# A fused adaLN block on one core: other DMA order, halos off GpSimd, wider value products, and DMA transposes instead of TensorE transposes

## The chip, the core and the metric

The kernel runs on one core of a Trainium2 chip. The core has TensorE (PE), whose results go to PSUM; VectorE (DVE) and ScalarE (ACT), which read PSUM and SBUF; GpSimd (POOL); and SyncE (SP), which here issues nearly all DMAs. Each engine works through its own list of instructions in order, and waits on semaphores for the others. A DMA is issued by an engine's queue and carried out by 16 DMA engines that all queues share.

The metric is the device time of one execution in microseconds (us). A profile is one more execution with the hardware profiler on; its span is the time from the first to the last instruction that it records.

## What is computed

The input x has 2048 rows (tokens) of 512 columns, in bf16. There are two residual parts, each scaled and shifted by rows that come from a vector c and a weight w_mod (`mod = silu(c) @ w_mod`, six rows of 512):

```python
h = layernorm(x) * (1 + ca) + sa
x = x + ga * A(h)            # local attention, then wo
h = layernorm(x) * (1 + cb) + sb
x = x + gb * B(h)            # an MLP over the tokens
```

A computes q, k and v (`h @ wqkv`, 32 heads of 16 columns). Each token attends to 8 tokens of its own head: itself and those 2, 4, ... 14 rows before it. So the logits are 8 elementwise products of q with shifted k, summed over the 16 columns of a head; then a softmax over the 8, and the weighted sum of 8 shifted v, followed by `@ wo`. B normalizes its input once more and multiplies over the token axis: `u = gelu(h^T @ w1 + b1)` with w1 of 2048 x 1792, `y = u @ w2 + b2` with w2 of 1792 x 2048.

## The kernel before

The work is staged in four chunks of 512 tokens (`build_chunk`, names ending in the chunk's number) and then the MLP.

One chunk goes through these steps. `ln1s` takes the statistics of 128 rows on DVE, `rstd1` and `nb1` make scale and offset, `ln1n` writes the normalized rows to the single buffer `n_sb`. `tr` transposes them, 16 blocks of 128x128 on PE into PSUM; `hT` applies `1 + ca` and `sa` on the way from PSUM to the SBUF buffer `hTb` (two chunks). `qkvq`, `qkvk`, `qkvv` are the products with the weights `w_raw`; `evq`, `evk`, `evv` evict them to `q_sb`, `k_c`, `v_c`. The tiles of k and v have 16 more columns ahead (the halo): `khalo` and `vhalo` copy them from the end of the chunk before, on GpSimd. `qk` forms the q·k products of all 8 shifts in one DVE instruction of 4096 columns (four per chunk, tile `prod`); `red` sums them on PE. `max`, `sub`, `exp`, `sum`, `rb`, `smul` are the softmax, and `a2` with its eviction lays the weights out anew. The values are laid out by 16 DMAs of 131 KB per chunk, SBUF to SBUF (`vd`, tile `vD`, three buffers). `pv` multiplies weights and values on DVE (tile `pvb`), `pvacc` sums on PE, `oev` evicts. `wo` is the product with wo plus the residual; `x1ev` and `x1sq` on ACT evict x and its sum and sum of squares; `mv2`, `rstd2`, `nb2`, `t`, `aff` are the second layer norm with scale and shift, `ln3s`, `rstd3`, `nb3`, `h3_` the normalization inside B.

The first MLP product has two levels over tokens, 0 to 1023 (level 0, possible after chunk 1) and 1024 to 2047. `ld_w1_0_f` and `ld_w1_1_f` load blocks f = 0 to 6 of w1, 512 KB each, into the four buffers `wst`. Level 0 is parked in `gT`, level 1 adds and applies gelu. The second product takes eight blocks of w2, `ld_w2_0` to `ld_w2_7` of 896 KB each, which reuse the buffers `hTb`, `prod`, `vD` and `pvb`.

The order of all this is not written by hand. Each step is entered in a graph with its engine or engines to choose from, an estimated duration, and what it reads and writes. `schedule` (line 100) is a list scheduler: it plays the estimates forward and takes, on each engine, the ready step with the lowest priority number; the numbers are the table `PRI` by name, plus 100 per chunk, and 1000 and more for the MLP. Steps that ACT and DVE can both do (evictions, `ln1n`, `t`, `h3_`, `hT`) go to the one that would finish first by the estimates. The instructions are then emitted in the planned order, and each engine's list stays in that order. DMAs on SP's list are in that order too. In the built program a DMA also waits until the DMA issued eight places before it has landed.

All instructions show one line in the profile (L201, the wrapper that issues them), so the work is told apart by tiles.

## Time and profile before

| | us |
|---|---|
| median of 3 runs | 228.56 (228.03 to 229.26) |
| profiled execution | 229.36 |
| its span | 227.4 |
| PE busy | 197.9 |
| DVE busy | 163.5 |
| ACT busy | 118.2 |
| GpSimd busy | 17.2 |

Slices on the page are 5.7 us each, counted here from 0. The attention of the four chunks fills the span up to about 130 us, the first MLP product runs from about 100 to 174, the second from 174 to 223. A matmul's end is modelled, so for dense work the distance from start to start (0.22 us for 512 columns) is a better duration than the one in the table (0.38). "Idle before" names what ended the idle time ahead of an instruction.

### The profile page before, as it was taken

To read this page: it belongs to the slowest core of one execution; us is meant where nothing else is said; L and a number is where in the kernel's file an instruction comes from. 1 tells how busy PE (TensorE), PEld (TensorE's weight loads), DVE (VectorE), ACT (ScalarE), POOL (GpSimd) and SP (SyncE) were. 2 spreads that over 40 slices of the span, in tenths; PEclk is the share of its full clock that TensorE was granted. 3 is DMA by queue.
4 is the path that set the end of the run, shared out by engine and by line. 5 is a ranking of instruction groups with operands and counts; after the bars stand their busy time and mean duration, and the time that the engine had idled before them with its cause. 6 is when DMAs were issued, how large, how long until landed. Compare 5 with 4: busy or idle time off the path is not lost.

```text
span 227.4 us, 3331 instructions
## 1 busy us (share of the span) xinstructions
PE 197.9 (87%) x1241; PEld 88.6 (39%) x1261; DVE 163.5 (72%) x232; ACT 118.2 (52%) x212; POOL 17.2 (8%) x33
## 2 busy tenths in 40 slices
PE   0279989979998999669289999989999999999992
PEld 0234544444453334323124334434344444444440
DVE  4634999999999999996993989972624444455552
ACT  2334894688679899893167966864634200000000
POOL 7000000010029700000000000000000000000000
PEclk9999999999999999958969999999999999999999
DMA  4999879857519510437999799970800011110111
GB/s 150 348 332 213 253 205 260 213 151 115 167 49 167 165 27 0 128 86 219 206 170 226 194 299 291 290 217 10 248 23 0 23 46 49 46 36 33 50 46 46
DMA packets 40884, 32.96 MB, mean 145 GB/s; under 512 B 1956, under 2 KB 37796, under 8 KB 40868
## 3 DMA queue, kind: packets, MB, share of 16 engines
q1 hardware_dynamic: 40860, 32.75, 57.1%
q8 instruction: 10, 0.16, 0.3%
q14 instruction: 6, 0.05, 0.1%
q10 hardware_dynamic: 8, 0.00, 0.0%
HBM read 22.03 MB, written 2.10 MB: 106 GB/s over the span
## 4 chain that ended last, share of the span: by engine, by line
PE 60%; DVE 17%; DMA 12%; ACT 5%; issue 3%; SPq 1%; DVEq 0%; ACTq 0%
PE ps L201 60%; DVE prod L201 6%; DMA wst<-in_B_w_dram 6%; DVE pvb L201 6%; DMA vD<-in_w_mod_dram 4%; DMA vD<-v_c 3%; ACT hTb L201 2%; ACT v_c L201 1%; SPq L201 1%; DVE h L201 1%; ACT q_sb L201 1%; DVE st L201 1%; DVE k_c L201 1%; DVE ee L201 1%; DVE nm L201 0%
## 5 line engine op out<-in xcount | busy, mean ns | idle before, releaser
L201 PE MATMUL ps<-h,wst 128*128 128x512 bf16 x218 | 52.6, 394 | 1.7 <-DMA wst<-in_B_w_dram 1.1
L201 PE MATMUL ps<-hTb,w_raw 128*128 128x512 bf16 x187 | 46.8, 393 | 2.2 <-ACT hTb L201 0.8
L201 DVE TENSOR_TENSOR pvb<-a2sb,vD 128x2048 bf16<-128x2048 bf16 x32 | 37.2, 1217 | 4.0 <-ACT a2sb L201 3.9
L201 DVE TENSOR_TENSOR prod<-q_sb,k_c 128x4096 bf16<-128x4096 bf16 x16 | 36.3, 2281 | 0.0
L201 PEld LDWEIGHTS <-wst 128*128 128x128 bf16 x224 | 21.7, 101 | 32.2 <-issue 7.5
L201 PEld LDWEIGHTS <-w_raw 128*128 128x128 bf16 x192 | 20.9, 116 | 26.1 <-issue 8.8
L201 PEld LDWEIGHTS <-vD 128*128 128x128 bf16 x132 | 10.6, 100 | 20.1 <-DMA vD<-in_w_mod_dram 7.9
L201 PE MATMUL ps<-gT,vD 128*128 128x512 bf16 x82 | 18.2, 379 | 0.1
L201 PE MATMUL ps<-woq,o_sb 128*128 128x512 bf16 x60 | 16.1, 380 | 0.2
L201 PE MATMUL ps<-prod,group 128*32 128x512 bf16 x128 | 10.7, 413 | 5.2 <-DVE prod L201 5.2
L201 DVE SCALAR_TENSOR_TENSOR q_sb<-ps,b2col,gb_bc 128x512 f32<-128x512 f32 x8 | 6.0, 750 | 12.6 <-PE ps L201 12.6
L201 DVE SCALAR_TENSOR_TENSOR k_c<-ps,b2col,gb_bc 128x512 f32<-128x512 f32 x8 | 6.0, 750 | 12.4 <-PE ps L201 12.4
L201 PE MATMUL ps<-pvb,stack 128*32 128x512 bf16 x128 | 10.3, 391 | 5.2 <-DVE pvb L201 4.7
L201 POOL COPY v_c<-v_c 128x64 bf16<-128x64 bf16 x3 | 12.0, 4005 | 26.1 <-ACT v_c L201 26.1
L201 ACT ACTIVATE hTb<-ps,sacol,a1col 128x512 bf16<-128x512 bf16 x13 | 9.4, 787 | 5.9 <-DVE hTb L201 5.4
L201 DVE TENSOR_TENSOR n_sb<-ps,gT 128x1024 f32<-128x1024 f32 x4 | 4.9, 1224 | 10.4 <-PE ps L201 8.2
L201 PE MATMUL ps<-gT,prod 128*128 128x512 bf16 x55 | 12.2, 379 | 0.1
L201 PE MATMUL ps<-gT,pvb 128*128 128x512 bf16 x55 | 12.2, 379 | 0.1
L201 DVE BATCH_NORM_STATS2 st<-xx 128x6 f32<-128x512 bf16 x16 | 10.7, 671 | 1.0 <-DMA xx<-in_A_x_dram 1.0
L201 ACT ACTIVATE q_sb<-ps 128x1024 bf16<-128x1024 f32 (+1 forms) x8 | 7.3, 913 | 7.2 <-PE ps L201 7.2
L201 ACT ACTIVATE xx<-ps 128x512 bf16<-128x512 f32 x16 | 9.4, 590 | 2.8 <-PE ps L201 2.2
L201 DVE BATCH_NORM_STATS2 st<-h 128x6 f32<-128x512 bf16 x16 | 10.7, 671 | 0.1
(92 smaller groups left out, 233.8 us busy)
## 6 DMA issues: line engine op xcount, KB each, us to landing
vD<-v_c SPq DMA_DIRECT2D x64, 131.5 KB, 4.0
wst<-in_B_w_dram SPq DMA_DIRECT2D x14, 512.0 KB, 5.3
vD<-in_B_w_dram SPq DMA_DIRECT2D x3, 896.0 KB, 7.8
wst<-in_w_mod_dram SPq DMA_DIRECT2D x4, 512.0 KB, 9.9
prod<-in_B_w_dram SPq DMA_DIRECT2D x2, 896.0 KB
pvb<-in_B_w_dram SPq DMA_DIRECT2D x2, 896.0 KB, 8.9
xx<-in_A_x_dram SPq DMA_DIRECT2D x3, 512.0 KB, 13.4
vD<-in_w_mod_dram SPq DMA_DIRECT2D x1, 1024.0 KB, 8.4
```

The costliest lines, as they stand in the source:

```text
L201: r = fn(*a, **k)
```

## The change

Seven things change.

1. The estimates and the table `PRI` are new, so the order of the steps changes on every engine. A new kind of dependency (`behind`) orders a step behind others in the plan without a wait on the chip.
2. At the start, a one-column DVE copy (`hold_w`) into `w_raw` makes the load of the q and k weights wait for the first block of x. The other weight loads are ordered behind it. Three of the four wo loads come ahead of it.
3. In chunk 0, the PE transposes go to two PSUM tiles instead of one, one evicted by DVE and one by ACT.
4. In chunks 1 to 3, `n_sb` is transposed by four DMAs on SP (128 rows of 512 columns each) straight into `hTb`; scale and shift are then applied in place, SBUF to SBUF, on DVE or ACT. The code for this was there (`TRD`), but not switched on.
5. The halo copies run on ACT or DVE; in the built program all six are on ACT.
6. The value products take 4096 columns in one instruction instead of two of 2048, 16 instead of 32 in all. The second layer norm's small operations are five fewer, and the normalizations use scale and offset as `x * rs + nb`.
7. The loads of w2 and of w1's level 1 are ordered behind the value copies of chunk 3. Blocks 0 to 2 of level 1 go to `w_raw`, which is free by then, instead of `wst`.

```diff
-    TRD: int = 0,
+    TRD: int = 1,
...
+    add("dve", 0.07, lambda: nc.vector.tensor_copy(w_raw[:, 0, 0:1], xx[:, 0, 0:1]), reads=[("xx", 0)], writes=["w_qk"],
+        name="hold_w", lat=0.1, pk=-200.0)
     dma(w_raw[:, :, 0:2 * D], wqkv_view[:, :, 0:2 * D], 2 * D * D * 2, [], ["w_qk"], "ld_wqk")
-    dma(w_raw[:, :, 2 * D:3 * D], wqkv_view[:, :, 2 * D:3 * D], D * D * 2, [], ["w_v"], "ld_wv")
+    first = [G.ops[-1]]
+    dma(w_raw[:, :, 2 * D:3 * D], wqkv_view[:, :, 2 * D:3 * D], D * D * 2, [], ["w_v"], "ld_wv", behind=first)
...
         if ch == 0 or not TRD:
-            stp = G.slot("ps")
+            stp = [G.slot("ps") for _ in range(2)]
...
+                if ch == 0:
+                    alts = [alts[1 - kp]]
...
         else:
             for sl in range(TPC):
                 add("sp", 0.7, lambda sl=sl: nc.sync.dma_start_transpose(hT[:, :, sl * P:(sl + 1) * P], n_sb[:, sl, :]),
...
-            add("pool", 0.9, lambda: nc.gpsimd.tensor_copy(k_c[b][:, :, 0:PAD], k_c[1 - b][:, :, C:C + PAD]),
-                reads=[("k", 1 - b, j) for j in range(4)], writes=[("khalo", b)], name=f"khalo{ch}")
-            add("pool", 0.9, lambda: nc.gpsimd.tensor_copy(v_c[b][:, :, 0:PAD], v_c[1 - b][:, :, C:C + PAD]),
-                reads=[("v", 1 - b, j) for j in range(4)], writes=[("vhalo", b)], name=f"vhalo{ch}")
+            for (nm_, t_) in (("k", k_c), ("v", v_c)):
+                G.add_any([("act", 0.25, lambda t_=t_: nc.scalar.activation(
+                               t_[b][:, :, 0:PAD], t_[1 - b][:, :, C:C + PAD], ACT.Identity)),
+                           ("dve", 0.15, lambda t_=t_: nc.vector.tensor_copy(
+                               t_[b][:, :, 0:PAD], t_[1 - b][:, :, C:C + PAD]))],
...
-                add("dve", _tt2(4 * C), f, reads=[("a2sb", b, wp)] + [("vD", vs, w4, dq % 2) for w4 in range(4)],
-                    writes=[("pv", pp)], name=f"pv{ch}_{dq}{wp}", lat=0.08)
+            def f(pp=pp, vs=vs, dq=dq):
+                av = _ap(a2sb[b][:, 0, 0:1], [[C, 2], [0, 4], [1, C]])
+                vv = _ap(vD[vs][:, 4 * (dq % 2), 8:9], [[-8, 2], [PAD + C, 4], [1, C]])
+                nc.vector.tensor_tensor(pvb[:, 2 * pp:2 * pp + 2, :, :], av, vv, op=ALU.mult)
...
-                nc.vector.tensor_scalar(me2[b][:, g0:g1], su2[b][:, g0:g1], 1.0 / D, None, op0=ALU.mult)
-                nc.vector.scalar_tensor_tensor(va2[b][:, g0:g1], me2[b][:, g0:g1], -1.0, me2[b][:, g0:g1],
+                nc.vector.scalar_tensor_tensor(va2[b][:, g0:g1], su2[b][:, g0:g1], float(D) ** -2, su2[b][:, g0:g1],
                                                op0=ALU.mult, op1=ALU.mult)
...
+            if last and fc < 3:
+                w = ("wr", fc)
+                w1p = w_raw[:].rearrange("p a b -> p (a b)")[:, fc * 2048:fc * 2048 + nst * EW].rearrange(
+                    "p (a b) -> p a b", a=nst)
...
-        dma(w2p, w2_view[:, :, sc2 * SW:(sc2 + 1) * SW], P * NFT * SW * 2, [], wkeys, f"ld_w2_{sc2}")
+        dma(w2p, w2_view[:, :, sc2 * SW:(sc2 + 1) * SW], P * NFT * SW * 2, [], wkeys, f"ld_w2_{sc2}",
+            behind=last_vd[-16:], rate=290.0)
```

On SP's list of the built program, the four transposes of chunk 1 and those of chunk 2 stand among the 16 value copies of chunk 0, those of chunk 3 among the value copies of chunk 1. The loads of w1's level-0 blocks 1 to 3 stand behind the value copies of chunk 0.

## The prediction

> **What bounds the kernel now.** I read the page's busy shares and slices first, then the busy times by stage, then the chain of waits against TensorE's (PE's) own timeline, then VectorE's (DVE's).
>
> ```profile
> PE 197.9 (87%) x1241; PEld 88.6 (39%) x1261; DVE 163.5 (72%) x232; ACT 118.2 (52%) x212; POOL 17.2 (8%) x33
> ...
> PE   0279989979998999669289999989999999999992
> ...
> DVE  4634999999999999996993989972624444455552
> ...
> PEclk9999999999999999958969999999999999999999
> ```
>
> PE is busy 87% of the span and idle for 29.5 us in all; DVE is near full in slices 4 to 17. By stage (columns: length, then busy time of PE, PE weight load, DVE, ACT, GpSimd, then granted PE clock, DMA share, GB/s):
>
> ```profile
> 30.00:45.00 15.00, 14.38 (x86) 6.40 (x87) 14.53 (x19) 10.04 (x15) 0.24 (x1) 1.00 1.01 248
> ...
> 75.00:90.00 15.00, 14.89 (x91) 6.31 (x90) 14.66 (x19) 13.58 (x28) 2.94 (x1) 1.00 0.26 64
> 90.00:99.80 9.80, 6.28 (x79) 2.86 (x77) 9.62 (x13) 8.67 (x20) 0.00 (x0) 0.89 0.34 95
> 99.80:115.00 15.20, 9.96 (x61) 3.93 (x58) 12.76 (x18) 6.87 (x12) 0.00 (x0) 0.84 0.85 192
> ...
> 125.00:134.00 9.00, 8.85 (x57) 3.33 (x57) 8.86 (x13) 7.09 (x20) 0.00 (x0) 1.00 0.91 234
> ```
>
> Until about 100 us DVE is full and PE nearly so. From 90 to 115 PE is idle for 3.5 + 5.2 = 8.8 us, waiting for DVE's products, and after those idle stretches the granted clock sinks. From 115 on PE is full: the kernel ends as soon as PE has done what was left at that point.
>
> The chain of waits seems to say otherwise: it shows a weight load of 8.24 us near the end.
>
> ```profile
> 142.24 8.24 DMA wst<-in_B_w_dram
> ```
>
> PE's timeline (start, length, work, idle ahead of it) shows that this load cost PE only 0.55 us, since PE worked on other blocks meanwhile; a second one cost 0.58.
>
> ```profile
> 150.53 13.99 PE L201 MATMUL ps<-h,wst 128*128 128x512 bf16 x62 [0.55 <-DMA wst<-in_B_w_dram]
> 165.09 9.46 PE L201 MATMUL ps<-h,wst 128*128 128x512 bf16 x43 [0.58 <-DMA wst<-in_B_w_dram]
> ```
>
> So the time is set by when DVE has finished the attention of chunks 0 to 2, and by PE's remainder then. DVE's timeline has the marks I count by: first q·k product, first of chunk 1, the scaling of chunk 3's softmax (end 120.2, called X here), and the wait behind it.
>
> ```profile
> 26.01 2.26 DVE L201 TENSOR_TENSOR prod<-q_sb,k_c 128x4096 bf16<-128x4096 bf16 x1
> ...
> 43.55 2.27 DVE L201 TENSOR_TENSOR prod<-q_sb,k_c 128x4096 bf16<-128x4096 bf16 x1
> ...
> 119.62 0.68 DVE L201 TENSOR_TENSOR ee<-ee,rb 128x1024 bf16<-128x1024 bf16 x1
> 124.20 8.03 DVE L201 TENSOR_TENSOR pvb<-a2sb,vD 128x2048 bf16<-128x2048 bf16 x7 [3.90 <-ACT a2sb L201]
> ```
>
> In sum: 43.55 to the first product of chunk 1, 76.7 from there to X (2.4 of it idle), 107.2 from X to the end of the span: 227.4.
>
> **The change part by part.** Costs come from these groups (count, busy us, mean ns), taken start to start where instructions overlap:
>
> ```profile
> L201 DVE TENSOR_TENSOR pvb<-a2sb,vD 128x2048 bf16<-128x2048 bf16 x32 | 37.2, 1217 | 4.0 <-ACT a2sb L201 3.9
> L201 DVE TENSOR_TENSOR prod<-q_sb,k_c 128x4096 bf16<-128x4096 bf16 x16 | 36.3, 2281 | 0.0
> ...
> L201 ACT ACTIVATE hTb<-ps,sacol,a1col 128x512 bf16<-128x512 bf16 x13 | 9.4, 787 | 5.9 <-DVE hTb L201 5.4 <-PE ps L201 0.5
> ...
> L201 PE MATMUL ps<-ident,n_sb 128*128 128x128 bf16 x64 | 5.1, 242 | 0.0
> ```
>
> *Wider products.* 32 products of 2048 columns start every 1.15 us, 16 of 4096 columns every 2.20 us (the prod row, same size): 36.8 against 35.2, DVE −1.6. Five small operations of the layer norm go: −0.9. One PSUM eviction moves to ACT and a q eviction comes earlier.
>
> *Halos off GpSimd.* Six copies, 13.2 us of GpSimd in all (one took 11.1 us at 66.8), go to ACT. None is on the path: the slow one is used first by the value copies of chunk 3 at 104.9. Nothing queues behind them on GpSimd. On ACT the nearest row (128x128, 0.27 to 0.31 us) makes 1.6 us; ACT loses 4 us of hT work in the same stages, and that covers it. Without this cover ACT, 27.0 of 30 us busy from 60 to 90, would pass it on.
>
> *w2 behind the value copies.* Three w2 loads (2.7 MB) stood ahead of chunk 3's value copies on SP; the copies landed at 112.42 and DVE took them at 112.41, having done layer-norm work until then. DVE gains at most 0.1; PE's gap there (4.7 us) shrinks only as far as DVE's marks move. But the w1 loads now follow with w2 from about 114 on, see the rivals.
>
> *Start.* The w_qkv loads wait for the first x (hold_w), so the 1 MB of w_mod, landed at 10.2, competes with less: with x and three wo loads 1.9 MB, of which 0.9 are moved by 6 us; at the 293 to 396 GB/s of 6 to 10 us the rest is there at 8.8. Behind the waiting load on SP stand w_v and x of chunks 1 to 3, so these come no earlier. hT of chunk 0 then runs on DVE and ACT side by side (0.54 and 0.79 each) instead of alternating (12.99 to 15.74): last hT at 13.1, last QKV matmul of chunk 0 at 24 instead of 27.1. DVE's statistics need x of chunk 1, at 15.95 in the trace and about 16.0 here (0.4 MB of wo moved ahead of it); eight at 0.80 lead to the first product at 22.5 instead of 26.0.
>
> *DMA transposes for chunks 1 to 3.* PE loses 48 transposes, three blocks of 0.99 us: −3.0. SP gains 12 issues, and eight of these stand between the value copies of chunk 0, which wait for ACT's second v eviction (28.3; here 27.1). The last transpose that chunk 1 needs has nine issues ahead of it; at the 0.63 us of a value copy it starts at 32.8. Its landing is not in the trace. Nearest rows:
>
> ```profile
> DMA to landing us min/median/max: 2.7/4.0/6.8
> ...
> vD<-v_c SPq DMA_DIRECT2D x64, 131.5 KB, 4.0
> ...
> woq<-in_A_wo_dram SPq DMA_DIRECT2D x4, 128.0 KB, 9.2
> ```
>
> The value copy has the same size, source and target memory: 2.7, 4.0 or 6.8 us; the wo loads of 128 KB bound it from above at 9.2. I take 4.0, the same kind of transfer. So chunk 1's data is there at 36.8, ACT has scaled it by 39.0 (three at 0.71), where before QKV of chunk 1 began at 31.99. PE is idle for some 8 us from 30 on and restarts at half clock, as at 98 to 104. Queued behind: the last q·k product's reduction stands behind q of chunk 1 on PE (41.9), DVE's maximum behind that (43.1). On ACT a layer-norm write waits for a transpose to have read its buffer, so the last transpose of chunk 2 starts at 39.7 and lands at 43.7; DVE's hT of chunk 2 stands ahead of its q eviction (45.9); ACT's k eviction is done at 46.9. First product of chunk 1: 47.0 instead of 43.55. Between 22.5 and 47.0 DVE has 19.7 us of work, so 4.9 of stalls; of the 19.7, 2.5 are hT, norm and eviction work that ACT did before, or DVE later.
>
> *From there.* The built program's order of DVE's work up to X, with durations from the rows: 12 q·k and 12 value products at 2.20 (52.8), three maxima at 1.15, four scalings at 0.60, two affine steps at 2.39, eight statistics at 0.80, small operations 1.1, six hT and norm operations at 0.33: 72.9, and 1.0 of idle time, mostly at chunk 3's maximum, which waits behind MLP matmuls on PE. 73.9 instead of 76.7.
>
> *PE's remainder at X.* 52 MLP matmuls are done then instead of 44 (8 x 0.22 = −1.8), and the weight waits of 1.1 go if the loads are in time: 104.4 instead of 107.2.
>
> Sum: 47.0 + 73.9 + 104.4 = 225.3 against 227.4, −2.1. The profiled execution took 229.36, 1.96 more than its span and 0.8 above the median of 228.56; on the median the forecast is 226.5.
>
> **Rivals.** *Transposes late (slower).* Every us of landing beyond 4.0 counts about twice, since two transposes follow one another through ACT; from about 5.1 us the change loses. At 9.2 it is +10.4, so 236.9; if they go one after another at 4.0 each, the sixth lands at 22.4 + 24.0 = 46.4, +9.6, nearly the same: 236. For it: the DMA engines are already at a share of 1.01 from 30 to 45. Against it: three w1 loads (1.5 MB) leave that stage. The Trainium skill, "VectorE: DVE Perf Modes", section on the three transpose paths, gives 1309 ns for 128x128 by DMA against 390 ns on TensorE; one after another that is 5.2 us an instruction as an estimate, six of them from 22.4 on end at 53.6, 16.8 later than in my sum, and the time would be 243. "Advanced Engine Details and Errata", section X-Bar Transpose, has transposes as fast as plain DMAs, and by it the sum stays as it is. No run here shows either yet.
>
> *Transposes quick (faster).* At 2.7 us the first product of chunk 1 comes at 45.0: 224.5; with no stall at all at 42.2: 221.7. For it: the start's gain is then kept.
>
> *Weights late (slower).* PE needs w1 block 5 at X + 14 = 135. Ahead of it and with it are 5.4 MB from 114.5 on: 18.6 us at 291 GB/s (134 to 141.2), 23.1 at the 234 of 125 to 134, plus 2 to land: 135 to 139.6. In the second case PE, in order, waits 4.5: 231.0. It decides from 280 GB/s down.
>
> **Numbers.** Forecast 226.5 (own range 225 to 228): 0.42. Quick transposes, 224: 0.22. Weights late, 231: 0.13. Transposes late, 229 to 243: 0.23, of which 0.08 for one after another. About 0.5%, 1.1 us, is what a measurement tells from no change. Faster than 227.4: 0.22 and seven tenths of the forecast's 0.42, 0.51; same: the rest of the forecast, 0.13; slower: 0.36. The range cuts a tenth at either end: 222 to 235.
>
> **What would show it.** The transposes' landing near 4 us and the first q·k product of chunk 1 near 47; PE idle for about 8 us ahead of it; X near 121 and PE without gaps over 1 us from X on. The first product at 26 would refute the start; weight waits of some us after 130 the remainder; transposes of more than 5 us the sign. An ACT or DVE stall that I did not trace between 47 and 121 would move X directly.

## The result

The changed kernel takes 242.18 us (median, 241.26 to 242.70) against 228.56: a ratio of 1.059, with a 95% interval of 1.0558 to 1.0623. It is 13.6 us slower. The forecast was 226.5 us with a range of 222 to 235, so both the sign and the range were wrong. The profiled execution took 241.26 us, its span is 239.2.

These are busy shares and slices (now 6.0 us each) on the page of the changed kernel:

```profile
PE 204.0 (85%) x1213; PEld 86.8 (36%) x1213; DVE 161.6 (68%) x216; ACT 117.3 (49%) x214; POOL 4.0 (2%) x27
...
PE   0259944698999779995969999999999999999992
...
DVE  4427996448999498999996688968444444444442
...
PEclk9999995589999958998697999999999999999998
```

The hole is in slices 5 to 7 (30 to 48 us): PE sinks to 4 to 6 tenths, and the granted clock to 5. Before, PE stood at 8 or 9 there. A second, smaller hole is in slices 13 and 14, from 78 to 90 us, and the clock sinks again from slice 18 to 21. VectorE (DVE), which was full from slice 4 to 17, now has slices at 4 and 6 tenths.

VectorE's timeline of the changed kernel has the prediction's marks: the first q·k product, the wait for the transposes of chunk 1, the first product of chunk 1, the wait for the transposes of chunk 3, and the scaling whose end is called X.

```profile
25.61 2.26 DVE L204 TENSOR_TENSOR prod<-q_sb,k_c 128x4096 bf16<-128x4096 bf16 x1
...
43.23 0.41 DVE L204 TENSOR_SCALAR hTb<-hTb,a1col,sacol 128x512 bf16<-128x512 bf16 x1 [3.52 <-DMA hTb<-n_sb]
...
55.82 2.29 DVE L204 TENSOR_TENSOR prod<-q_sb,k_c 128x4096 bf16<-128x4096 bf16 x1 [1.11 <-ACT k_c L204]
...
83.66 1.06 DVE L204 TENSOR_SCALAR hTb<-hTb,a1col,sacol 128x512 bf16<-128x512 bf16 x3 [3.39 <-DMA hTb<-n_sb]
...
134.81 0.69 DVE L204 TENSOR_TENSOR ee<-ee,rb 128x1024 bf16<-128x1024 bf16 x1
```

From these marks the time falls into four stretches. Such a table was made for every run below; X is counted 0.6 us after the start of the last scaling.

| us | to first q·k product | from there to first of chunk 1 | from there to X | X to the end | span |
|---|---|---|---|---|---|
| kernel before | 26.0 | 17.5 | 76.7 | 107.2 | 227.4 |
| forecast | 22.5 | 24.5 | 73.9 | 104.4 | 225.3 |
| changed kernel | 25.6 | 30.2 | 79.6 | 103.8 | 239.2 |
| miss | +3.1 | +5.7 | +5.7 | -0.6 | +13.9 |

The last stretch came out as forecast. The other three were all too long: 3.1 at the start, 5.7 on the way to chunk 1 and 5.7 from there to X. These need separate causes.

Why the transposes of chunk 1 come late can be read from the SP queue's timeline of the changed kernel (start, length of the issue, what is issued). The order of the transposes is: chunk 1 first, chunk 1 second, chunk 2 first, chunk 1 third, chunk 2 second, chunk 1 fourth (38.96), chunk 2 third, chunk 2 fourth (46.75), then the four of chunk 3.

```profile
26.35 1.31 SPq L204 DMA_TRANSPOSE hTb<-n_sb  x1
...
30.88 1.20 SPq L204 DMA_DIRECT2D vD<-v_c  x2
32.17 1.22 SPq L204 DMA_TRANSPOSE hTb<-n_sb  x1
33.45 0.58 SPq L204 DMA_DIRECT2D vD<-v_c  x1
34.09 1.61 SPq L204 DMA_TRANSPOSE hTb<-n_sb  x1
...
37.06 1.21 SPq L204 DMA_TRANSPOSE hTb<-n_sb  x1
...
38.96 1.27 SPq L204 DMA_TRANSPOSE hTb<-n_sb  x1
...
46.75 1.21 SPq L204 DMA_TRANSPOSE hTb<-n_sb  x1
...
66.07 1.20 SPq L204 DMA_TRANSPOSE hTb<-n_sb  x1
...
79.06 1.25 SPq L204 DMA_TRANSPOSE hTb<-n_sb  x1
```

And these are the landings, from the page's list of DMA issues of the same kernel (last column: median us from issue to landing):

```profile
vD<-v_c SPq DMA_DIRECT2D x64, 131.5 KB, 4.4
...
hTb<-n_sb SPq DMA_TRANSPOSE x12, 4.2
```

In the median a transpose lands in 4.2 us, and the forecast had 4.0. But one occupies the queue for 1.2 to 1.6 us where 0.63 was assumed, and the fourth of chunk 1 leaves at 38.96 instead of 32.8. From 30.88, when the first value copy can leave, to that issue SP does not pause: the queue itself is what holds it.

### The profile page after: what moved, and what is told of

Its sections match the earlier page's. It is cut to its first block, busy times and chain, and to the rows that moved or that the text cites. A ratio compares the mean times of both kernels' runs of the same rounds, so it can differ in the third digit from the quotient of the medians.

```text
span 239.2 us, 3237 instructions
## 1 busy us (share of the span) xinstructions
PE 204.0 (85%) x1213; PEld 86.8 (36%) x1213; DVE 161.6 (68%) x216; ACT 117.3 (49%) x214; POOL 4.0 (2%) x27
## 2 busy tenths in 40 slices
DMA packets 47410, 34.51 MB, mean 144 GB/s; under 512 B 8484, under 2 KB 44324, under 8 KB 47396
## 4 chain that ended last, share of the span: by engine, by line
PE 48%; DVE 17%; DMA 15%; ACT 7%; issue 6%; SPq 5%; DVEq 0%; ACTq 0%
PE ps L204 48%; DMA hTb<-n_sb 6%; SPq L204 5%; DVE pvb L204 5%; DMA w_raw<-in_A_wqkv_dram 4%; DVE prod L204 4%; DMA wst<-in_B_w_dram 4%; DVE st L204 3%; DVE h L204 2%; ACT n_sb L204 2%; ACT hTb L204 2%; ACT h L204 1%; DMA xx<-in_A_x_dram 1%; DVE nm L204 1%; ACT v_c L204 1%
## 5 line engine op out<-in xcount | busy, mean ns | idle before, releaser
L204 PE MATMUL ps<-hTb,w_raw 128*128 128x512 bf16 x192 | 50.2, 412 | 4.8 <-DMA w_raw<-in_A_wqkv_dram 2.5
L204 PE MATMUL ps<-h,wst 128*128 128x512 bf16 x176 | 43.7, 394 | 2.9 <-ACT h L204 2.1
L204 PEld LDWEIGHTS <-w_raw 128*128 128x128 bf16 x240 | 25.9, 114 | 38.5 <-issue 15.8
L204 DVE TENSOR_TENSOR pvb<-a2sb,vD 128x4096 bf16<-128x4096 bf16 x16 | 36.0, 2288 | 4.2 <-ACT a2sb L204 2.9
L204 PEld LDWEIGHTS <-wst 128*128 128x128 bf16 x176 | 16.7, 99 | 27.6 <-issue 9.8
L204 PE MATMUL ps<-woq,o_sb 128*128 128x512 bf16 x64 | 17.3, 394 | 3.0 <-ACT xx L204 3.0
L204 PE MATMUL ps<-prod,group 128*32 128x512 bf16 x128 | 12.6, 484 | 7.6 <-DVE prod L204 7.6
L204 ACT ACTIVATE n_sb<-xx,nb,rs 128x512 bf16<-128x512 bf16 x13 | 10.1, 805 | 6.9 <-DMA hTb<-n_sb 6.4
L204 PE MATMUL ps<-h,w_raw 128*128 128x512 bf16 x48 | 10.8, 379 | 0.0
L204 ACT ACTIVATE v_c<-ps 128x1024 bf16<-128x1024 f32 x8 | 8.0, 1018 | 5.1 <-PE ps L204 5.1
```

The source lines that it names most:

```text
L204: r = fn(*a, **k)
```

## Experiments

Unless said otherwise, a kernel is the changed one with one edit, and the order of everything else is held fixed, so that marks can be compared. "Rest of the order" means the new priorities apart from the transposes. Kernels with the same start differ among their profiled executions by up to 2.3 us in the first mark (25.6 to 27.9, with the loading of the first weights), so the later marks are compared as distances. These differ too: five kernels with chunk 3's transposes in the same place show 77.6 to 79.6 us for the third stretch, and the profile of the changed kernel is the longest of them. The medians are therefore the better measure of a gain.

### Is it the transposes?

**The transposition left out.** The twelve DMAs are not issued, and scale and shift read `n_sb`:

```diff
-                add("sp", 0.7, lambda sl=sl: nc.sync.dma_start_transpose(hT[:, :, sl * P:(sl + 1) * P], n_sb[:, sl, :]),
+                add("sp", 0.7, lambda: None,
...
-                            hT[:, kt, :], hT[:, kt, :], a1col[:, kt:kt + 1], sacol[:, kt:kt + 1], op0=ALU.mult,
+                            hT[:, kt, :], n_sb[:, kt, :], a1col[:, kt:kt + 1], sacol[:, kt:kt + 1], op0=ALU.mult,
```

> The changed kernel in its own order with no DMA transposes at all: scale and shift read the normalized rows where they stand, so the transposition of chunks 1 to 3 is left out. It is the most that faster transposes could give. Theory Q (nearly the whole loss is the transposes' issue, place and landing): first q.k product of chunk 1 at 43 to 45 us instead of 55.8, no wait of DVE before chunk 3's scale and shift (3.4), 224 to 229 us. Rival P (half or more of the loss lies in the new order of the other work): 231 us or more.

Measured: 232.21 us (231.29 to 233.45), ratio to before 1.0164 (1.011 to 1.0217). So the transposes cost 10.0 of the 13.6 us. VectorE's timeline of this run:

```profile
27.53 2.26 DVE L204 TENSOR_TENSOR prod<-q_sb,k_c 128x4096 bf16<-128x4096 bf16 x1
...
47.24 1.23 DVE L204 TENSOR_REDUCE nm<-ps 128x128 bf16<-128x1024 f32 x1 [3.09 <-PE ps L204]
...
52.28 2.29 DVE L204 TENSOR_TENSOR prod<-q_sb,k_c 128x4096 bf16<-128x4096 bf16 x1 [1.73 <-ACT k_c L204]
...
76.68 1.05 DVE L204 TENSOR_SCALAR hTb<-n_sb,a1col,sacol 128x512 bf16<-128x512 bf16 x3
...
125.91 0.68 DVE L204 TENSOR_TENSOR ee<-ee,rb 128x1024 bf16<-128x1024 bf16 x1
```

The stretches are 27.5, 24.7, 74.2 and 104.9. The third stretch is what I had forecast (73.9), and the wait at chunk 3's scale and shift is gone. The second comes out at the forecast's 24.5 as well, but that is luck: the forecast counted 4.9 us of stalls in it, which it put down to the transposes, and 19.7 without them. Here there are no transposes, and VectorE still waits 4.8 us, 3.09 ahead of the maximum and 1.73 for the k eviction. So these stalls belong to the new order, and in the changed kernel the transposes come on top of them (30.2 - 24.7 = 5.5). The number lies in rival P's range, but by shares theory Q is nearer: the transposes are most of the loss, and there is a rest of 3.7 us beside them.

**Plain copies in their place.** The same bytes, the same place in the queue, but not transposed:

```diff
-nc.sync.dma_start_transpose(hT[:, :, sl * P:(sl + 1) * P], n_sb[:, sl, :])
+nc.sync.dma_start(hT[:, :, sl * P:(sl + 1) * P], n_sb[:, sl, :].rearrange("p (a b) -> p a b", a=KT))
```

> The changed kernel with each of the 12 DMA transposes replaced by a plain DMA of the same bytes in the same place; the transposition is left out, the order of all engines is the same. Theory Q: the issue takes 0.6 instead of 1.25 us, the landing stays near 4 us; the first q.k product of chunk 1 comes at 51 to 53 instead of 55.8 and the time is 237 to 239 us. Theory X: the landing falls below 3 us as well, value copies land sooner, the first product comes before 50 and the time is below 236. Rival P: 241 to 243, nothing changes.

Measured: 235.72 us (234.17 to 237.00), ratio 1.0324 (1.0252 to 1.0396). The list of DMA issues of this run has the landing:

```profile
hTb<-n_sb SPq DMA_DIRECT2D x12, 128.0 KB, 4.1
```

Its SP queue's timeline has the fourth of chunk 1, of chunk 2 and of chunk 3:

```profile
37.46 0.65 SPq L204 DMA_DIRECT2D hTb<-n_sb  x1
...
44.52 0.65 SPq L204 DMA_DIRECT2D hTb<-n_sb  x1
...
72.31 0.65 SPq L204 DMA_DIRECT2D hTb<-n_sb  x1
```

And VectorE's timeline has its scale and shift of chunk 2, released by the fourth copy, and of chunk 3:

```profile
47.58 0.74 DVE L204 TENSOR_SCALAR hTb<-hTb,a1col,sacol 128x512 bf16<-128x512 bf16 x2 [0.68 <-DMA hTb<-n_sb]
...
78.55 1.06 DVE L204 TENSOR_SCALAR hTb<-hTb,a1col,sacol 128x512 bf16<-128x512 bf16 x3 [3.21 <-DMA vD<-v_c]
```

The issue takes 0.65 us instead of 1.2 to 1.6, so the fourth of chunk 1 leaves 1.5 us earlier and the fourth of chunk 2 2.2 us earlier. In the median a plain copy lands no sooner, 4.1 us against 4.2. But the fourth of chunk 2, which is on the path and stands behind six value copies, released VectorE 3.1 us after its issue (44.52 to 47.58), where the transpose took 5.8 (46.75 to 52.51). The two make 4.9 us, and by that much the first product of chunk 1 is earlier (50.89). So theory X is right for one transfer and wrong for the median, and its range held the total. The second stretch shrinks from 30.2 to 24.9, which is all that leaving the transposition out gave there. The third does not shrink (80.4): chunk 3's fourth copy stands behind 12 value copies as before, and VectorE waits 3.21 us at 78.55. The profile names a value copy as the releaser of that wait; scale and shift read only what the four copies wrote, so I take it for the fourth, 6.2 us after its issue. VectorE waits another 1.66 us, at 88.20, for a value copy. So there seem to be two costs, that of the transposing form at chunks 1 and 2, and the place in the queue at chunk 3; the second is tested by itself below.

**TensorE transposes in the changed kernel.** `TRD` back to 0; here the planner orders all steps anew.

```diff
-    TRD: int = 1,
+    TRD: int = 0,
```

> The changed kernel with the transposes of chunks 1 to 3 back on TensorE; everything else of the change stays, the planner orders the steps anew. Theory Q (the DMA transposes leave late, because of their place and length in SP's queue) and theory X (a transposing transfer is slow and slows the others) both expect 222 to 229 us, at or below the kernel before. Rival P (the new order of the work costs the time, whatever transposes) expects 235 us or more.

Measured: 244.76 us (243.20 to 245.53), ratio 1.07 (1.0622 to 1.0778). That is what rival P expected, but it does not bear rival P out for the changed kernel, because the order is not that of the changed kernel any more. PE's timeline shows a place that no other run has:

```profile
163.06 11.72 PE L204 MATMUL ps<-h,w_raw 128*128 128x512 bf16 x35 [7.50 <-ACT h L204]
```

PE waits 7.5 us for the last normalization of chunk 3, since the attention of that chunk was planned late. Its loss lies after X: 119.1 us against 103.8. The run shows only that this table of priorities does not suit TensorE transposes. The run above, with the order held, answers the question.

**The DMA transposes alone, in the order of the kernel before.** Four transposes are issued where TensorE's stood, ahead of the value copies:

```diff
 # kernel before
                 def f(g0=g0, g1=g1):
+                    if ch > 0:
+                        for sl in range(g0, g1):
+                            nc.sync.dma_start_transpose(hT[:, :, sl * P:(sl + 1) * P], n_sb[:, sl, :])
+                        return
                     for kt in range(KT):
...
-                    return trp()[:, kt * C:(kt + 1) * C]
+                    return trp()[:, kt * C:(kt + 1) * C] if ch == 0 else hT[:, kt, :]
```

> The kernel before, in its own order, with nothing but the transposes of chunks 1 to 3 turned into four DMA transposes each, issued where TensorE's stood, ahead of the value copies, and scale and shift applied in place. Theory Q: the four of chunk 1 are issued in 5 us from about 26 on and land 4.2 us later, near 35; QKV of chunk 1 starts 4 to 5 us later than 32.0, the other chunks lose 0 to 2 us each and TensorE gains 3: 229 to 234 us. Theory X: four at a time land in 6 us or more and the value copies behind them are slowed: 235 or more. Rival P: no loss, 225 to 229.

Measured: 236.02 us (235.68 to 236.25), ratio 1.0339 (1.0283 to 1.0394): DMA transposes cost 7.5 us in the old order too. The SP queue's timeline of this run has the four of chunk 1 and the four of chunk 2:

```profile
24.19 6.08 SPq L201 DMA_TRANSPOSE hTb<-n_sb  x4
...
46.14 5.92 SPq L201 DMA_TRANSPOSE hTb<-n_sb  x4
```

This is its list of DMA issues:

```profile
vD<-v_c SPq DMA_DIRECT2D x64, 131.5 KB, 5.2
...
hTb<-n_sb SPq DMA_TRANSPOSE x12, 3.8
```

And this is VectorE's wait for them in chunk 2, from its timeline:

```profile
55.12 0.41 DVE L201 TENSOR_SCALAR hTb<-hTb,a1col,sacol 128x512 bf16<-128x512 bf16 x1 [2.28 <-DMA hTb<-n_sb]
```

Four in a row take 6 us to issue. In the median they land in 3.8 us, less than theory X had said. The value copies take 5.2 in the median instead of 4.0, but that can't be put down to the transposes: in a run below that has none (the kernel before with fewer small operations) they take 5.0. The second stretch grows by only 2.0 us (19.5), less than theory Q had said, and the third by 5.3 (82.0), more than it had said. VectorE's waits between chunk 1 and X are 7.3 us against 2.3 before. The total lies in theory X's range (235 or more), without the long landing that this theory gives as the reason, and nothing in it speaks for rival P.

### Where in the queues?

**Two transposes of chunk 1 moved ahead.** After planning, SP's list is changed by a small helper, `ahead(names, mark)`, which moves steps to just before another:

```diff
+    order = ahead(("tr1_2", "tr1_3"), "vd0_000")
```

> The changed kernel with the third and fourth transpose of chunk 1 moved ahead of the value copies of chunk 0 in SP's queue; nothing else changes. Theory Q: the fourth leaves at 33 instead of 39.0, chunk 1's data is there at 37 instead of 43.1, its first product comes 4 to 6 us earlier and the time is 236 to 238.5 us. Theory X: with four transposes under way together the landing grows from 4.2 to over 6 us and less than 2 us are gained. Rival P: less than 1 us.

Measured: 242.18 us (241.80 to 242.43), ratio 1.0608 (1.0551 to 1.0666): nothing gained. That is rival P's number. But the median landing stayed at 4.0 us, so theory X does not explain it. ScalarE's (ACT's) timeline of this run does:

```profile
43.48 0.81 ACT L204 ACTIVATE n_sb<-xx,nb,rs 128x512 bf16<-128x512 bf16 x1 [2.77 <-DMA hTb<-n_sb]
44.20 2.21 ACT L204 ACTIVATE hTb<-hTb,sacol,a1col 128x512 bf16<-128x512 bf16 x3
```

The fourth transpose now leaves near 33.4, 5.5 us earlier, but on ACT the scale and shift of chunk 1 (44.20) stand behind a normalization of chunk 3 (43.48). That one waits for a transpose of chunk 2 to have read its place in `n_sb`. The single buffer `n_sb` ties three chunks together: a wait that was hidden behind the late transpose comes up in its place.

**Both queues put right for chunks 1 and 2.** The normalizations of chunk 3 go behind chunk 1's scale and shift, and six value copies behind chunk 2's last transpose:

```diff
+    order = ahead(("tr1_2", "tr1_3"), "vd0_000")
+    order = ahead(("ln1n12", "ln1n13"), "ln1n14")
+    order = ahead(("vd0_100", "vd0_110", "vd0_120", "vd0_130", "vd0_101", "vd0_111"), "vd0_121")
```

> The changed kernel with the third and fourth transpose of chunk 1 ahead of the value copies, with ACT's two normalizations of chunk 3 moved behind its scale and shift of chunk 1, and with six value copies moved behind the last transpose of chunk 2. Theory A (in the run before, ACT's queue took the gain: a normalization of chunk 3, waiting for a transpose of chunk 2 to have read its buffer, stood ahead of chunk 1's scale and shift): chunk 1's first product comes 29 minus 3 to 5 us after the first q.k product, 25 to 27 instead of 30.2, 237.5 to 239.5 us. Rival: DVE's own part of the scale and shift, behind the third product of chunk 0, holds it in any case, less than 1.5 us gained, 240.5 or more.

Measured: 237.08 us (236.30 to 238.47), ratio 1.0406 (1.0356 to 1.0456), 5.1 less than the changed kernel. The second stretch is 24.6 us (26.60 to 51.21 in VectorE's timeline), the same as with no transposition at all. Theory A holds; it had expected a little less gain (237.5 to 239.5).

**Chunk 3's transposes ahead of chunk 1's value copies.**

```diff
+    order = ahead([o.name for o in order if o.name.startswith("vd1_0") or o.name in ("vd1_100", "vd1_110", "vd1_120", "vd1_130")], "vd1_101")
```

> The changed kernel with the last three transposes of chunk 3 issued right behind the first, ahead of the value copies of chunk 1 instead of between them; nothing else moves. Theory Q (place in SP's queue): the fourth leaves at 71 instead of 79.1 and lands by 76, DVE's wait of 3.4 us ahead of chunk 3's scale and shift goes, and with it PE's idle 3 us and restart: the way from chunk 1's first product to X shrinks from 79.7 to 75 to 76, 238 to 239 us. Rival (the copies of chunk 1, now 4 us later, hold the value products instead): 241 or more.

Measured: 237.63 us (237.27 to 239.66), ratio 1.0442 (1.039 to 1.0494), 4.6 less. VectorE's scale and shift of chunk 3 follows the product before it without a wait:

```profile
78.54 2.29 DVE L204 TENSOR_TENSOR prod<-q_sb,k_c 128x4096 bf16<-128x4096 bf16 x1
80.74 1.06 DVE L204 TENSOR_SCALAR hTb<-hTb,a1col,sacol 128x512 bf16<-128x512 bf16 x3
```

The third stretch falls from 79.6 (77.6 to 79.0 in the other kernels with the old place) to 74.2, as with no transposition. The value copies of chunk 1, now later, hold nothing.

### The start, and the parts by themselves

**The wo loads behind the weights.** The hold writes elsewhere, and the three wo loads return to their old place:

```diff
-    add("dve", 0.07, lambda: nc.vector.tensor_copy(w_raw[:, 0, 0:1], xx[:, 0, 0:1]), reads=[("xx", 0)], writes=["w_qk"],
+    add("dve", 0.07, lambda: nc.vector.tensor_copy(junk[:, 0:1], xx[:, 0, 0:1]), reads=[("xx", 0)], writes=["w_qk"],
...
+    order = ahead(("ld_wo0", "ld_wo1", "ld_wo2"), "ld_wo3")
```

> The changed kernel with the hold on the weight loads taken off and the three wo loads moved back behind the loads of w_qkv and x, the start as it was before; transposes as in the changed kernel. Theory W (at the start, QKV of chunk 0 waits for its weights, issued 2.9 us later behind the wo loads): weights land by 14, chunk 0's last QKV matmul ends at 27 or earlier instead of 28.0, the transposes behind the value copies go 1 us or more earlier, 239.5 to 241.2 us. Rival (the start is hidden behind the wait for the transposes): 241.5 to 242.8.

Measured: 239.44 us (238.49 to 239.86), ratio 1.0471 (1.0434 to 1.0507), 2.7 less than the changed kernel. PE's timeline at the start, of the changed kernel:

```profile
10.27 1.01 PE L204 MATMUL ps<-sc,vD 128*128 128x1 bf16 x32 [7.90 <-DMA vD<-in_w_mod_dram]
...
14.59 0.61 PE L204 MATMUL ps<-hTb,w_raw 128*128 128x512 bf16 x1 [1.58 <-DMA w_raw<-in_A_wqkv_dram]
16.10 11.91 PE L204 MATMUL ps<-hTb,w_raw 128*128 128x512 bf16 x47 [0.89 <-DMA w_raw<-in_A_wqkv_dram]
```

and of this run:

```profile
9.20 1.01 PE L204 MATMUL ps<-sc,vD 128*128 128x1 bf16 x32 [6.82 <-DMA vD<-in_w_mod_dram]
...
12.15 0.58 PE L204 MATMUL ps<-hTb,w_raw 128*128 128x512 bf16 x1 [0.21 <-DVE hTb L204]
13.39 12.51 PE L204 MATMUL ps<-hTb,w_raw 128*128 128x512 bf16 x47 [0.66 <-DMA w_raw<-in_A_wqkv_dram]
```

In the changed kernel PE waits 1.58 us for the weights of q and k. They were issued at 5.17, behind the three wo loads, and not at 2.31 as before. The second wait, 0.89 us, is not the change's: behind the first weight load, the next follows after a pause of 1.39 us in the changed kernel (14.59 to 16.09), in this run (11.88 to 13.39) and in the kernel before (12.97 to 14.47). The hold itself cost nothing in the changed kernel, as it was done at 3.9 while SP issued the wo loads until 5.13; this run takes both away, so it does not price the hold without them. With the old place weights, w_mod and chunk 1's x (VectorE's statistics begin at 14.88 instead of 17.58) are all earlier, and the first product comes at 23.5. Theory W holds.

**Halos back on GpSimd.** The six copies move to GpSimd at the same place in the order:

```diff
-                G.add_any([("act", 0.25, lambda t_=t_: nc.scalar.activation(
-                               t_[b][:, :, 0:PAD], t_[1 - b][:, :, C:C + PAD], ACT.Identity)),
+                G.add_any([("act", 0.25, lambda t_=t_: nc.gpsimd.tensor_copy(
+                               t_[b][:, :, 0:PAD], t_[1 - b][:, :, C:C + PAD])),
```

> The changed kernel with the six halo copies back on GpSimd at the same place in the order. My prediction (the halos are free on either engine): 242.2 within 0.6. Rival H (a GpSimd copy of up to 11 us, as before, holds the value copies that read the halo): chunk 2's or chunk 3's value copies leave later, 243 to 248.

Measured: 242.17 us (240.75 to 243.01), against 242.18. In this kernel the halos are free on either engine. The longest copy took 3.1 us here, not 11.

**The wide products in the kernel before.** The first of two steps forms both products, the second nothing:

```diff
 # kernel before
                 def f(wp=wp, pp=pp, off=off, vs=vs, dq=dq):
-                    nc.vector.tensor_tensor(pvb[:, pp, :, :], a2sb[b][:, wp, :].unsqueeze(1).to_broadcast([P, 4, C]),
-                                            vD[vs][:, 4 * (dq % 2):4 * (dq % 2) + 4, off:off + C], op=ALU.mult)
+                    if wp == 1:
+                        return
+                    av = _ap(a2sb[b][:, 0, 0:1], [[C, 2], [0, 4], [1, C]])
+                    vv = _ap(vD[vs][:, 4 * (dq % 2), 8:9], [[-8, 2], [PAD + C, 4], [1, C]])
+                    nc.vector.tensor_tensor(pvb[:, pp:pp + 2, :, :], av, vv, op=ALU.mult)
```

> The kernel before with nothing but the 32 value products of 2048 columns merged into 16 of 4096. My prediction's term: DVE is shorter by 1.6 us and, since DVE sets the pace, so is the kernel: 226.5 to 227.5. Rival: PE gets its first values of a pair 1.1 us later and the gain is lost: 228 to 229.

Measured: 227.33 us (226.23 to 228.35), ratio 0.9955 (0.9929 to 0.9981): 1.1 us, near the forecast's 1.6.

**Fewer small operations on top.** The second layer norm as in the change:

```diff
 # kernel before, wide products
-                nc.vector.tensor_scalar(me2[b][:, g0:g1], su2[b][:, g0:g1], 1.0 / D, None, op0=ALU.mult)
-                nc.vector.scalar_tensor_tensor(va2[b][:, g0:g1], me2[b][:, g0:g1], -1.0, me2[b][:, g0:g1],
+                nc.vector.scalar_tensor_tensor(va2[b][:, g0:g1], su2[b][:, g0:g1], float(D) ** -2, su2[b][:, g0:g1],
...
-                nc.vector.tensor_tensor(va2[b][:, g0:g1], va2[b][:, g0:g1], sq2[b][:, g0:g1], op=ALU.add)
+                nc.vector.tensor_tensor(va2[b][:, g0:g1], sq2[b][:, g0:g1], va2[b][:, g0:g1], op=ALU.subtract)
```

> The kernel before with the wide products and the second layer norm's five fewer small operations, in its own order. By my prediction's terms (DVE sets the pace until about 115 us): 0.5 to 0.9 us less than the wide products alone, 226.2 to 227.0. Rival (those small operations stand beside waits for ACT): the same as the wide products alone, 227.3.

Measured: 226.31 us (225.67 to 227.51), ratio 0.9931 (0.9899 to 0.9962). It is faster than both kernels. The step from the wide products alone is 1.0 us between two medians that were not measured side by side, and the intervals of the two ratios overlap, so this step by itself is not shown.

**w2 behind the value copies, on top of that.**

```diff
 # kernel before, wide products, fewer small operations
+    order = ahead(("ld_w2_0", "ld_w2_1", "ld_w2_2"), "ld_w2_5")
```

> The kernel before with fewer DVE operations, and its first three w2 loads moved behind the value copies of chunk 3 in SP's queue. My prediction's step (DVE gains at most 0.1, the weights are still in time): 226.3 within 0.6. Rival V (the copies of chunk 3 land earlier and TensorE's wait of 4 us near 111 shrinks): 224.5 to 225.5. Rival L (weights late, as in my third rival): 227.5 or more, with waits of TensorE for wst or w2 after 130.

Measured: 234.39 us (233.75 to 235.10), ratio 1.0276 (1.0228 to 1.0325), 8.1 us slower than without this edit. PE's timeline of this run:

```profile
154.18 25.16 PE L201 MATMUL ps<-h,wst 128*128 128x512 bf16 x108 [6.22 <-DMA wst<-in_B_w_dram]
```

The same place in PE's timeline without the edit:

```profile
148.47 23.57 PE L201 MATMUL ps<-h,wst 128*128 128x512 bf16 x105 [0.48 <-DMA wst<-in_B_w_dram]
```

TensorE waits 6.2 us for w1 instead of 0.5, and that is 5.7 of the 7.1 us between the two spans. 2.7 MB of w2 now go ahead of two w1 blocks that come due first; these are issued from 126.46 instead of 119.05 on. This is my third rival, in the order of the kernel before. In the changed kernel it did not happen. There, level 1's first blocks go to `w_raw` and are issued among the first, at 127.65 to 131, and PE's only wait for weights after X is 0.55 us, in its timeline:

```profile
150.93 1.04 PE L204 MATMUL ps<-h,wst 128*128 128x512 bf16 x4 [0.55 <-DMA wst<-in_B_w_dram]
```

### All repairs together, and what is left

**All three repairs.** The moves of wo, of chunks 1 and 2, and of chunk 3 in one kernel:

```diff
+    order = ahead(("ld_wo0", "ld_wo1", "ld_wo2"), "ld_wo3")
+    order = ahead(("tr1_2", "tr1_3"), "vd0_000")
+    order = ahead(("ln1n12", "ln1n13"), "ln1n14")
+    order = ahead(("vd0_100", "vd0_110", "vd0_120", "vd0_130", "vd0_101", "vd0_111"), "vd0_121")
+    order = ahead([o.name for o in order if o.name.startswith("vd1_0") or o.name in ("vd1_100", "vd1_110", "vd1_120", "vd1_130")], "vd1_101")
```

> The changed kernel with both of these and with the wo loads back behind the weights. If the three causes are separate, the gains add: 242.2 - 2.7 - 3.5 - 3.5 = 232.5, between 231 and 234 us, still slower than before, since with no transposition at all and the start repaired it would be 232.2 - 2.7 = 229.5. Rival (they share one wait): 235 or more.

Measured: 230.09 us (229.74 to 230.51), ratio 1.0084 (1.0044 to 1.0123). That is below the expected range, since two gains had come out larger than the 3.5 counted for each. With the measured gains the sum is right: 242.2 - 2.7 - 5.1 - 4.6 = 229.8. The three causes are separate. The stretches are 24.0, 24.9, 75.3 and 104.0. Three of them are below those of the kernel before, and the second is 7.4 us longer. In it, by PE's timeline, PE waits for VectorE's second product:

```profile
35.87 1.04 PE L204 MATMUL ps<-prod,group 128*32 128x512 bf16 x8 [4.59 <-DVE prod L204]
```

VectorE's list has statistics of chunks 2 and 3 ahead of that product, and its part of chunk 1's scale and shift behind the third one, at 38.01. The next two runs move these.

**Scale and shift on VectorE ahead of the third product.**

```diff
+    order = ahead(("hT1_1",), "qk0_2")
```

> The changed kernel with all repairs, and DVE's part of the scale and shift of chunk 1 moved ahead of the third q.k product of chunk 0. Theory O (what is left of the loss is the order of DVE: this operation, 0.33 us long, stood behind a product of 2.2 us and with it QKV of chunk 1): QKV of chunk 1 starts 1.5 to 2.2 us earlier, DVE's waits of 2.96 and 1.94 us behind it shrink, 227.5 to 229.0 us. Rival (DVE's work, not its order, is what is left): 229.7 to 230.5.

Measured: 229.83 us (227.87 to 231.24), ratio 1.0076 (1.0039 to 1.0112): no gain that can be told. QKV of chunk 1 stands behind the sums of chunk 0's products in PE's own list as well (PE starts it at 39.78).

**Statistics of chunk 3 moved behind the products.** On top of the run before:

```diff
+    order = ahead(("ln1s13", "ln1s14", "ln1s15", "rstd1_3_0", "nb1_3_0"), "ln1n12")
+    order = ahead(("hT1_1",), "qk0_3")
```

> The run before, with three of the four statistics of chunk 3 (2.4 us of DVE) and the scale and offset that follow from them moved behind the last q.k product of chunk 0, where DVE waited 2.7 us for TensorE. Theory D (what is left of the loss is DVE's order: statistics of chunks 2 and 3 stand ahead of chunk 0's products, TensorE waits 4.6 us for the second product with QKV of chunk 1 behind it in its own list): second product 2.4 us earlier, DVE's wait of 2.7 us filled with work, first product of chunk 1 at 45.5 to 46.5 instead of 48.2, 227.0 to 228.3 us. Rival (the wait for TensorE ahead of the maximum only moves elsewhere): 229.5 or more.

Measured: 230.01 us (229.42 to 231.08), ratio 1.0062 (1.0034 to 1.009). The second product came 1.4 us earlier, and VectorE's wait of 2.7 us shrank to 0.4, as theory D said. But the first product of chunk 1 still came at 48.40. ACT's timeline shows where the wait went:

```profile
41.11 0.30 ACT L204 ACTIVATE lv<-mv,epscol 128x4 f32<-128x4 f32 x1 [5.08 <-DVE mv L204]
```

ACT now waits 5.08 us for the moved statistics, with the normalizations of chunk 3 and the q eviction of chunk 1 behind them in its list. The rival holds: the wait moved. So what is left over the kernel before lies in the second stretch, which is 24.7 us long without any transposition too, but two moves in VectorE's list did not lower it. Whether another order would, stays open; in the run with TensorE's transposes, planned anew, this stretch took 17.5 us, as in the kernel before, and the loss came later.

## Why the prediction was wrong

*What bounds the kernel.* Right. Time followed VectorE's marks up to X and PE's remainder after it in every run whose order was held: from X to the end, the eleven kernels with the changed order took 103.7 to 104.9 us.

*Start (forecast: first product 3.5 us earlier).* Wrong by 3.1 us in this profile, and by up to 5.4 in others with the same start; the step is the term for QKV of chunk 0. I followed w_mod and hT and let QKV start with the last hT at 13.1. I left out that the weights of q and k, too, were moved in the queue, behind three wo loads; they landed at 14.57 (5.17, and 9.4 in the page's list of DMA issues). Even w_mod came no earlier (PE began with it at 10.27, before 10.21). The DMA engines moved 260 GB/s from 8 to 10 us and not the 387 of the kernel before; my sum had used 293 to 396 from there, for another mix of loads. The x of chunk 1 was late too, at 17.58 instead of 16.0. The run with the wo loads moved back gave 2.7 us, and its first product came at 23.5, still 1.0 behind the forecast.

*DMA transposes.* The first product of chunk 1 came at 55.8 and not at 47.0. The 8.8 us are a sum. 3.7 come from the start: the value eviction that the copies between the transposes wait for ended at 30.8 instead of 27.1. 2.4 come from the issues, the term that I had mis-sized: I took 0.63 us for each, the duration of a value copy's issue, and a transpose's is 1.2 to 1.6. The landing of chunk 1's fourth was right (4.15 for 4.0); that of chunk 2's fourth was 1.7 longer (5.7). ACT added 0.8, one more normalization ahead of that transpose than I had counted. My rule that a us of landing counts twice was not tested, since only one of the two landings grew. One link I had missed, a normalization of chunk 3 ahead of chunk 1's scale and shift on ACT; it showed only when the transpose ahead of it was made early. A second failed step does not show in this sum: the 4.9 us of stalls up to chunk 1, which I charged to the landing of the transposes, remain (4.8) when nothing is transposed. They belong to the new order, and moving VectorE's statistics did not remove them. My 42.2 with no stall at all, for quick transposes, was therefore out of reach in this order.

*PE's gap.* I forecast 8 us of idle time from 30 on, ahead of chunk 1's QKV and because of its late data. PE was idle for 8.2 of the 15 us from 30 to 45, but the size is luck. PE's timeline of the changed kernel has the waits:

```profile
37.49 1.04 PE L204 MATMUL ps<-prod,group 128*32 128x512 bf16 x8 [4.59 <-DVE prod L204]
...
44.00 3.70 PE L204 MATMUL ps<-hTb,w_raw 128*128 128x512 bf16 x8 [2.37 <-ACT hTb L204]
```

5.8 us were waits for VectorE's second and third product (4.59, and 1.23 at 39.76), which the run without transposition has as well, and 2.37 for chunk 1's scale and shift. The granted clock from 30 to 45 was 0.71. PE's first eight QKV matmuls of chunk 1 took 3.70 us; eight later ones took 1.92.

*From chunk 1 to X (forecast 73.9 with 1.0 of idle time).* The work was right: without transposes this stretch took 74.2. The failed step is that I looked for transposes in the way at chunks 1 and 2 and not at chunk 3. Its four stand between 12 value copies in SP's list. The first left at 66.07, when TensorE had read `hTb` for the last time for chunk 1, the fourth 13.0 us later, and VectorE waited 3.39 us at 83.66. With PE's restart behind that, it cost 4.6 us by the medians (5.4 by this stretch of the two profiles); moving the three ahead of the copies removed it.

*Remainder (forecast 104.4).* Measured 103.8. The 1.1 us of weight waits became 0.55, and the weights were not late.

*Wide products, halos.* Right within 0.5 us: 1.1 of 1.6 us for the products, and the halos free on either engine. The small operations could not be told by themselves, and the two PSUM tiles of chunk 0 have no run of their own. *w2 behind the value copies* was costed at nothing. In the changed kernel that held. I put that down to the buffer of their own that the first blocks of level 1 got; no run takes it away. In the old order the same move cost 8.1 us.

*The rivals.* "Transposes late" was the case that came true, at 0.23, and its range of 229 to 243 held the result, which is luck in the main: its two mechanisms were not the ones measured. The landing was not long in the median (4.2, below the break-even of 5.1; only the one at 5.7 was above it), and the transposes did not go one after another: three left within 3.9 us in the run that issued them together, where the median landing was 4.0. What I had not listed is the price of a transpose in the queue that issues it. The estimate from the Trainium skill, "VectorE: DVE Perf Modes", 5.2 us for each instruction one after another, gave 243, close to the time, for a reason that the trace does not show. "Advanced Engine Details and Errata", section X-Bar Transpose, has transposes as fast as plain DMAs; the trace agrees for the landing (4.2 against 4.1 us) and not for the issue (1.25 against 0.65).

## What to carry to other kernels

A DMA has three prices: its time in the issuing queue, its time to land, and what stands behind it in that queue. Before costing a new kind of DMA, count the issues between it and its reader in the queue's list, and treat the length of its issue as unknown if no trace shows it. A load that is moved should be followed to every reader whose data it now goes ahead of, and a long wait that has been removed should be expected to uncover the next one in the same list.

## What was not expected of the hardware

- A DMA transpose of 128x512 in bf16, SBUF to SBUF, took 1.25 us to issue in the changed kernel (median; 1.20 to 1.61), a plain DMA of the same bytes in the same place 0.65 us. In the median both landed in about the same time, 4.2 and 4.1 us.
- Transposes use the DMA engines more per byte. In the stretch from 30 to 45 us (columns: length, then busy time of PE, weight load, VectorE, ScalarE, GpSimd, then granted clock, DMA share, GB/s) the changed kernel shows

```profile
30.00:45.00 15.00, 6.80 (x35) 2.46 (x35) 11.37 (x17) 7.19 (x12) 0.00 (x0) 0.71 1.20 169
```

  and the run with plain copies

```profile
30.00:45.00 15.00, 8.28 (x39) 2.96 (x39) 12.57 (x17) 9.11 (x15) 0.00 (x0) 0.77 0.85 212
```

  a share of 1.20 at 169 GB/s against 0.85 at 212. The packets are not smaller for it: the page of the changed kernel counts 8484 under 512 B and that of the plain copies 8293, where the kernel before has 1956. They take longer. Over the whole span, the pages show for the SP queue (packets, MB, time of the packets as a share of 16 engines' span), first of the changed kernel, then of the plain copies:

```profile
q1 hardware_dynamic: 47388, 34.32, 67.7%
```

```profile
q1 hardware_dynamic: 47196, 34.32, 60.7%
```

  That is 161.9 us of 239.2 against 142.6 of 235.0 for the same bytes. Without transposes or copies it is 59.6% of 231.4, 137.9. The time includes what packets wait for each other, so not all of the difference need be the transposes' own.
- The landing of value copies varies by more than transposes could be shown to add. In the kernel before with DMA transposes, the 16 copies of chunk 0 behind four transposes landed in 5.2 and 5.4 us (medians of eight), and in the kernel before with fewer small operations, with no DMA transposes, in 5.2 and 5.5; in the kernel before they took 4.7 and 3.3.
